# Half tiles for the first block's attention units, all their loads first, and a new order table, in an attention and mixing kernel

## The chip, the cores and the metric

The kernel runs on one core of a Trainium2 chip. The metric is the time of one execution on the device, in microseconds; lower is better. The median of runs is what counts, and one execution under the profiler gives the trace that is read here.

## What is computed

Three stages follow each other on 4 x 576 tokens of 512 features: windowed attention (8 heads of 64, each query sees itself and the 63 positions before it), a token-shift mixer with a squared relu and a sigmoid gate, and a convolution gate of five taps with two more products. All inputs are handed over in 64 bits.

```python
scores = scale * np.matmul(q, k.transpose(0, 1, 3, 2))
scores = np.where((rel >= 0) & (rel < 64), scores, -1e9)
attn = np.exp(scores - max); attn = attn / (sum + 1e-9)
x = attn @ v                                  # (4, 576, 512)
xk = mu_k * x + (1.0 - mu_k) * x_prev         # x_prev: one token back
xr = mu_r * x + (1.0 - mu_r) * x_prev
k = np.maximum(xk @ w_k, 0.0);  v = k * k @ w_v
x = sigmoid(xr @ w_r) * v
gate = sigmoid(causal 5-tap convolution of x with conv_w)
return (gate * (x @ w_val)) @ w_out
```

## The kernel before

**Tiles and stages.** The 2304 tokens are cut into five blocks (`BLOCKS`): block 0 of 256 tokens, blocks 1 to 4 of 512. For each block four attention units, one for each pair of heads, run qk on TensorE (L252, one PSUM buffer for all units), a mask on VectorE (L264), memsets of batch edges on POOL (`edge`, L274), a maximum (`top`, L282), exps with sums on ScalarE (L288), an epsilon add and a reciprocal (L292, L295), a normalization (L297), transposes (L305) and their copies (L311, L312), pv (L318) and a copy into xT (L324, L325). Then `mix` scales xT by mu (L355 on ScalarE or L360 on VectorE) and adds the shifted part with omu = 1 - mu (L371). From block 1 on, x is split into a high and a low part (L385 or L386, L388), and every product (r, h, v; L401) is three matmuls: high by high, high by low, low by high. Block 0 multiplies in one plain pass (L419). After block 4 come val and out, with the convolution taps (L540) on VectorE.

**Weights.** A weight arrives as 64-bit words in 1 MB pieces: two of w_r, four of w_k, four of w_v. `words` makes floats of them: ScalarE L186, a shift on VectorE (L189), a join on VectorE (L191). `weight` then takes the high part (`hi`, L212 on ScalarE or L213 on VectorE) and the rest (`lo`, L215 on VectorE). The first four pieces are loaded by SP (L208), the other six by instructions in ScalarE's queue (L205), each into a buffer that an earlier piece has left. Units load qk (L239) and v (L245) through SP, too; `small` loads mu and the convolution weights.

**What sets the order.** Nothing is reordered at run time: each engine runs its queue in order. Class `Plan` lists operations with a rank, an engine, an estimated duration and dependencies, and lays out a schedule with a model of its own: among the operations that could start on an engine within 130 ns of the earliest, the lowest rank goes first. The ranks come from the table `RANK`. `any` lets an operation go to the engine that ends it first, so a copy or a relu may be on ScalarE, VectorE or POOL. Where TensorE would wait for long early on, `fill` adds idle matmuls (L697). The numbers behind `moves` are the model's transfer times.

**Tiles of the units.** Each unit takes its own tiles qk, vt, s and m from the pool `at2`, which has two buffers of each, also in block 0, where a unit fills only half of one. So unit 2's load of qk waits for unit 0's matmuls (`back("qk", 2)`).

Of the kernel before, what the change touches and what calls it, by code (L numbers as in the profile page):

```python
# [10 lines left out]
I32 = mybir.dt.int32  # L11
# [16 lines left out]
TB = 512  # L28
# [6 lines left out]

RANK = {'first': -349, 'unit': 1, 'mix': -179, 'w_r': -619, 'w_k': -312, 'w_v': -49, 'halves': 300,
        'next': -241, 'nextstep': 74, 'att': -17, 'step': 24, 'inner': 4, 'ahead': 387, 'mixes': -83,
        'mixstep': 56, 'prep': 6, 'gate': 225, 'ldx': 188, 'w2': 65, 'out': 181}


class Plan:
# [5 lines left out]
    START, LAND = 500, 700  # L47
    RAMP, SLOW = 9000, 1.6
    WAIT, PASS = 700, 480
    TABLE = 1280  # L50

    def __init__(self, bias, **rings):

        self.ops, self.bias, self.rings, self.fill = [], bias, rings, None

    def op(self, key, eng, ns, rank, deps, fn, ring=None, table=None, moves=0):

        self.ops.append((rank, len(self.ops), key, ((eng, ns, fn),), deps, ring, table, moves))

    def any(self, key, rank, deps, *ways):  # L60

        self.ops.append((rank, len(self.ops), key, ways, deps, None, None, 0))

    def run(self):
        todo = sorted(self.ops, key=lambda o: o[:2])
        keys = {o[2] for o in todo}
        assert all(d in keys for o in todo for d in o[4])
        end, free, ready = {}, {}, {}
        used = {r: [] for r in self.rings}
        table = None  # L70
        link = 0
        while todo:
            can = {}
            for o in todo[:600]:
                rank, _, key, ways, deps, ring, tab, _ = o
                if key not in ready:
                    if any(d not in end for d in deps):
                        continue
                    ready[key] = max([end[d] + self.HOP for d in deps], default=0)
                t = ready[key]  # L80
# [5 lines left out]
                b = self.bias(rank)  # L86
                w = min(ways, key=lambda w: max(t, free.get(w[0], 0)) + w[1] + b.get(w[0], 0))
                t = max(t, free.get(w[0], 0)) + (self.TABLE if tab and tab != table else 0)
                can.setdefault(w[0], []).append((t, o[:2], o, w))
            assert can, ("no order", [o[2] for o in todo[:8]])  # L90
            t, _, o, w = min((min((c for c in cs if c[0] <= min(cs)[0] + self.SLACK), key=lambda c: c[1])
                              for cs in can.values()), key=lambda c: c[:2])
            _, _, key, _, deps, ring, tab, moves = o
            table = tab or table
            if w[0] == "pe" and self.fill and t - free.get("pe", 0) > self.WAIT:
                self.fill(t, int((t - max(free.get("pe", 0), 1500) - 250) // self.PASS))
            free[w[0]] = t + w[1]
            end[key] = t + w[1]
            if moves:
                link = max(link, end[key] + self.START) + moves * (self.SLOW if link < self.RAMP else 1)  # L100
                end[key] = link + self.LAND
            if ring:
                used[ring[0]].append(ring[1])
            todo.remove(o)
            w[2]()


@with_exitstack
def tile_kernel(ctx, tc, qkh, vh, mu, conv, w_k, w_v, w_r, w_val, w_out, out):
# [84 lines left out]
    def weight(key, rank, w_dram, dst, nm, bufs, prev=None, sprev=None, after=(), free=(), later=None, used=(), queue="dma"):  # L194
# [8 lines left out]
        if queue == "act":  # L203
            op((key, "ld"), "act", 60, rank - 1, [*after, *([(prev, "hi")] if prev else [])],
               lambda: ACT.dma_start(out=bufs()[0], in_=w_dram[key[1]].bitcast(I32)), moves=2.8 * n)  # L205
        else:
            op((key, "ld"), "dma", 420, rank - 1, [*after, *([(prev, "s")] if prev else [])],
               lambda: DMA.dma_start(out=bufs()[0], in_=w_dram[key[1]].bitcast(I32)), moves=2.8 * n)  # L208
        words(key, rank, n, raw, s, [(key, "ld")], [*used, *([(sprev, "lo")] if sprev else [])])
# [15 lines left out]
    def unit(u, r):  # L225
# [20 lines left out]
        op(("ldv", u), "dma", 420, r[3] - RANK["ahead"], back("pv", 2), load_v, moves=3.3 * n)  # L246

# [11 lines left out]
        def mask():  # L259
            s = a["s"] = tile_(at2, "s", [P, 2 * TB // P, P])[:, :2 * n2, :]  # L260
# [487 lines left out]
```

## Time and profile before

| | us |
|---|---|
| median of three runs (455.67 to 456.62) | 456.11 |
| the profiled execution | 454.78 |
| its span, first to last instruction | 453.0 |
| TensorE matmuls busy | 432.6 (95%) |
| VectorE busy | 309.4 (68%) |
| ScalarE busy | 234.3 (52%) |
| POOL busy | 12.2 (3%) |

Times in the views count from the start of the span. A busy share is an average over stages with different limits, so stages are read one by one. A matmul record (PE) ends at a modelled time, and weight loads (PEld) run beside it. Consecutive instructions on VectorE and ScalarE overlap a little: the next one starts before the row of the last has ended.

### The profile page before, as it was taken

The numbers are of one execution on the slowest core, as the hardware profiler recorded it, in microseconds if no ns is written. First come the engines' busy times: TensorE is split into PE (matmuls) and PEld (weight loads), VectorE is DVE, ScalarE is ACT, GpSimd is POOL, SyncE is SP. The second block draws the span as 40 slices with busy tenths as digits, with TensorE's granted clock in tenths as the row PEclk, the third lists the DMA queues.
The fourth block names the chain that finished last, engine by engine and source line by source line (L and its number), as shares of the span: only waits on it lengthen the run. The fifth ranks groups of instructions, "written<-read, shape, count | busy, mean of one in ns | idle before, by whom it ended". The sixth has DMA issues, their size and how long they took to land.

```text
span 453.0 us, 7977 instructions
## 1 busy us (share of the span) xinstructions
PE 432.6 (95%) x3242; PEld 373.0 (82%) x3242; DVE 309.4 (68%) x453; ACT 234.3 (52%) x536; POOL 12.2 (3%) x60
## 2 busy tenths in 40 slices
PE   7687999789999999999999999999999999999996
PEld 5565888678877887878888878888888999999996
DVE  3989999887569215789306946999611899995330
ACT  4667999584758213877046853547400543541122
POOL 2010000000000000001000000000000000000000
PEclk9988999989999999999999999999999999999999
DMA  8994923531113114123121004524041203110122
GB/s 292 415 357 154 341 62 112 167 99 46 48 48 100 48 49 141 51 69 125 69 71 47 1 2 151 186 93 139 1 150 57 95 28 132 53 54 27 52 80 104
DMA packets 16116, 48.90 MB, mean 108 GB/s; under 512 B 1872, under 2 KB 2640, under 8 KB 14800
## 3 DMA queue, kind: packets, MB, share of 16 engines
q1 hardware_dynamic: 15216, 42.10, 27.5%
q10 hardware_dynamic: 864, 6.29, 3.5%
q8 instruction: 25, 0.41, 0.4%
q14 instruction: 11, 0.09, 0.1%
HBM read 38.95 MB, written 9.44 MB: 107 GB/s over the span
## 4 chain that ended last, share of the span: by engine, by line
PE 91%; DVE 5%; issue 1%; ACT 1%; POOL 0%; ACTq 0%; POOLq 0%; DVEq 0%
PE h L401 20%; PE v L401 19%; PE out L401 11%; PE val L401 11%; PE r L401 10%; PE at L318 4%; PE qk L252 4%; PE h L419 3%; PE v L419 3%; PE at L305 3%; PE r L419 1%; PE idle L697 1%; DVE s L264 1%; DVE s L191 1%; DVE m L282 1%
## 5 line engine op out<-in xcount | busy, mean ns | idle before, releaser
L401 PE MATMUL h<-x,wk 128*128 128x512 f32 x384 | 92.4, 395 | 0.0
L401 PEld LDWEIGHTS h<-x,wk 128*128 128x128 f32 x384 | 70.7, 188 | 14.8 <-issue 0.2
L401 PE MATMUL v<-sh,wv 128*128 128x512 f32 x256 | 80.0, 390 | 0.0
L288 ACT ACTIVATE s<-s,m 128x128 f32<-128x128 f32 x144 | 55.7, 388 | 11.1 <-DVE m L282 11.1
L401 PEld LDWEIGHTS v<-sh,wv 128*128 128x128 f32 x256 | 48.1, 188 | 10.0
L401 PE MATMUL val<-x,wk 128*128 128x288 f32 x384 | 52.0, 294 | 0.0
L401 PEld LDWEIGHTS val<-x,wk 128*128 128x128 f32 x384 | 51.2, 188 | 0.1
L540 DVE SCALAR_TENSOR_TENSOR gate<-xb,wc,gate 128x576 f32<-128x576 f32 x64 | 48.8, 810 | 3.3 <-ACT gate L538 3.3
L401 PE MATMUL v<-sl,wv 128*128 128x512 f32 x128 | 49.8, 389 | 0.0
L401 PE MATMUL r<-x,wr 128*128 128x512 f32 x192 | 47.6, 401 | 0.0
L401 PEld LDWEIGHTS r<-x,wr 128*128 128x128 f32 x192 | 35.8, 191 | 7.9 <-issue 0.7
L501 DVE TENSOR_TENSOR sg<-v,sg 128x512 f32<-128x512 f32 (+1 forms) x20 | 12.7, 633 | 40.2 <-PE v L401 36.3
L252 PE MATMUL qk<-qk 64*64 64x128 f32 x576 | 22.5, 296 | 8.6 <-issue 4.5
L312 DVE COPY pt<-at 128x512 f32<-128x512 f32 (+1 forms) x17 | 11.5, 674 | 26.2 <-PE at L305 26.1
L538 ACT ACTIVATE gate<-xb,wc 128x576 f32<-128x576 f32 x16 | 11.2, 765 | 33.3 <-DMA xb<-x2d 33.3
L264 DVE SCALAR_TENSOR_TENSOR s<-qk,cap 128x1024 f32<-128x1024 f32 (+1 forms) x24 | 22.5, 953 | 8.2 <-PE qk L252 8.2
L401 PEld LDWEIGHTS v<-sl,wv 128*128 128x128 f32 x128 | 24.0, 188 | 4.9
L252 PEld LDWEIGHTS qk<-qk 64*64 64x64 f32 x576 | 17.1, 143 | 13.3 <-issue 7.2
L447 ACT ACTIVATE rk<-h 128x512 f32<-128x512 f32 (+1 forms) x29 | 16.2, 565 | 22.6 <-PE h L401 21.4
L288 ACT ACTIVATION_READ_ACCUMULATOR s<-s,m 128x1 f32 x144 | 26.9, 187 | 0.0
L401 PE MATMUL out<-g1h,wk 128*128 128x288 f32 x128 | 26.9, 295 | 0.0
L401 PE MATMUL out<-g0h,wk 128*128 128x288 f32 x128 | 26.9, 295 | 0.0
(113 smaller groups left out, 681.9 us busy)
## 6 DMA issues: line engine op xcount, KB each, us to landing
qk<-qk SPq DMA_DIRECT2D x16, 544.0 KB, 4.6
vt<-vh SPq DMA_DIRECT2D x16, 512.0 KB, 3.8
xb<-x2d SPq DMA_DIRECT2D x4, 1152.0 KB, 5.9
out_t<-o SPq DMA_DIRECT2D x15, 288.0 KB, 2.1
x2d<-sg SPq DMA_DIRECT2D x16, 256.0 KB, 2.0
raw<-w_r SPq DMA_DIRECT2D x2, 1024.0 KB, 8.6
raw<-w_k ACTq DMA_DIRECT2D x2, 1024.0 KB, 8.1
raw<-w_v ACTq DMA_DIRECT2D x2, 1024.0 KB, 7.2
```

The lines of the kernel that those rows point to most:

```text
L252: PE.matmul(a["ps"][heads[c % 2], h, c // 2 * P:c // 2 * P + P], lhsT=a["q"][heads[h], c * W:(c + 1) * W], rhs=a["k"][heads[h], c * W:c * ...
L264: V.scalar_tensor_tensor(out=o, in0=ps[:, i:i + j], scalar=D ** -0.5, in1=cap[:, None, :].to_broadcast([P, j, P]), op0=ALU.mult, op1=ALU.min)
L288: ACT.activation(out=s, in_=s, func=AF.Exp, bias=l(0)[:, c:c + 1], accum_out=l(1)[:, c:c + 1])
L305: PE.transpose(a["tp", h][:, c * P:(c + 1) * P], a["s"][:, h * n2 + c, :], ident)
L312: ("dve", v_ns(n), lambda h=h: V.tensor_copy(a["pt"][:, h, :n], a["tp", h][:, :n])))
L318: PE.matmul(a["o"][heads[h], c * W:(c + 1) * W], lhsT=a["v"][:, c, heads[h]], rhs=a["pt"][:, h, c * W:(c + 1) * W], start=True, stop=True)
L401: PE.matmul(ps, lhsT=a, rhs=b[:, kt, :], start=(kt == 0 and i == 0), stop=(kt == nk - 1 and i == 2))
L419: PE.matmul(Ps[key][:, :n], lhsT=ws(kt), rhs=x()[:, kt, :], start=kt == 0, stop=kt == nk - 1)
L447: ACT.activation(out=o, in_=ps, func=AF.Relu)
L501: V.tensor_tensor(out=s, in0=Ps["v", t, m][:, :n], in1=s, op=ALU.mult)
L538: ACT.activation(out=g, in_=src, func=AF.Copy, scale=c)
L540: V.scalar_tensor_tensor(out=g, in0=src, scalar=c, in1=g, op0=ALU.mult, op1=ALU.add)
```

## The change

The four units of block 0 now share tiles in pairs: `half` gives an even unit a new tile and the odd one its second half, so two buffers hold all four units, and their eight loads wait for nothing. `back2` states the new dependencies: none in block 0; the first two units of block 1 wait for both units of the pair whose tile they take. The tile qk is 64 columns wider, so that two halves fit. mu has a load of its own with rank -1000 that depends on the load of unit 0's v; the convolution weights keep theirs. The planner has lost an unused argument, finds ready operations in another way, and has other constants for transfers. `RANK` has other numbers, and a new table `ADJ` adds a number to the rank of 27 single operations.

```diff
-RANK = {'first': -349, 'unit': 1, 'mix': -179, 'w_r': -619, 'w_k': -312, 'w_v': -49, 'halves': 300,
+RANK = {'first': -329, 'unit': 14, 'mix': -497, 'w_r': -234, 'w_k': -132, 'w_v': 138, 'halves': 542,
...
+ADJ = {('exp', 7): 265, ('mask', 15): -40, ('r', 0, 3): -195, (('w_v', 3), 't'): -390, ('h', 2, 1): 40,
...
-    RAMP, SLOW = 9000, 1.6
+    RAMP, SLOW = 7500, 1.6
...
-        self.ops.append((rank, len(self.ops), key, ((eng, ns, fn),), deps, ring, table, moves))
+        self.ops.append((rank + ADJ.get(key, 0), len(self.ops), key, ((eng, ns, fn),), deps, ring, table, moves))
...
-    def small():
-        DMA.dma_start(out=sm, in_=mu)
-        DMA.dma_start(out=cw, in_=conv.bitcast(I32).rearrange("p (n t) -> p n t", t=2))
-    op("ldc", "dma", 840, -180, [("ldqk", 1)], small, moves=100)
-    op("omu", "dve", 70, -160, ["ldc"],
+    op("ldmu", "dma", 420, -1000, [("ldv", 0)], lambda: DMA.dma_start(out=sm, in_=mu), moves=100)
+    op("ldc", "dma", 420, -180, [("ldqk", 1)],
+       lambda: DMA.dma_start(out=cw, in_=conv.bitcast(I32).rearrange("p (n t) -> p n t", t=2)), moves=100)
+    op("omu", "dve", 70, -960, ["ldmu"],
...
+        def back2(k):
+
+            return [] if t == 0 else [(k, 2 * (u - HP) + i) for i in range(2)] if u < HP + 2 else [(k, u - 2)]
...
+        def half(tag, shape):
+
+            if t:
+                return tile_(at2, tag, shape)
+            if hp % 2 == 0:
+                Q["half", tag] = tile_(at2, tag, shape)
+            return Q["half", tag][:, hp % 2 * shape[1] // 2:]
...
-            both = tile_(at2, "qk", [P, 2 * TB + W])
+            both = half("qk", [P, 2 * TB + 2 * W])
...
-        op(("ldqk", u), "dma", 420, r[0] - RANK["ahead"], back("qk", 2), load_qk, moves=3.2 * n)
+        op(("ldqk", u), "dma", 420, r[0] - RANK["ahead"], back2("qk"), load_qk, moves=2.9 * n)
...
-            a["v"] = tile_(at2, "vt", [P, TB // W, P])
+            a["v"] = half("vt", [P, TB // W, P])
...
-        op(("mask", u), "dve", v_ns(n * 2), r[1], [("qk", u), "cap", *back("mask", 1), *back("tp", 2)], mask)
+        op(("mask", u), "dve", v_ns(n * 2), r[1], [("qk", u), "cap", *back("mask", 1), *back2("tp")], mask)
...
-        l = lambda i: a["m"][:, 8 * i:8 * i + 2 * n2]
+        l = lambda i: a["m"][:, n2 * 2 * i:n2 * 2 * (i + 1)]
```

The order of instructions follows. Names are tiles, the number tells one buffer from another; a count at the end (x2) is of equal rows in a row.

The queue of SP from its start, before: units 0 and 1, then the weights, then unit 2.

```order
L239 DMA qk_129<-qk 128x576
L239 DMA qk_131<-qk 128x576
L245 DMA vt_133<-vh 128x512
L245 DMA vt_135<-vh 128x512
L208 DMA raw_112<-w_r 128x2048
L208 DMA raw_113<-w_r 128x2048
L208 DMA x_110<-w_k 128x2048
L208 DMA s_111<-w_k 128x2048
L239 DMA qk_158<-qk 128x576
L171 DMA sm<-mu 128x8
L172 DMA cw<-conv 128x40
```

The same queue after the change:

```order
L264 DMA qk_110<-qk 128x576 x2
L264 DMA qk_132<-qk 128x576
L270 DMA vt_134<-vh 128x512
L264 DMA qk_132<-qk 128x576
L270 DMA vt_134<-vh 128x512
L270 DMA vt_143<-vh 128x512 x2
L220 DMA raw_114<-w_r 128x2048
L220 DMA raw_115<-w_r 128x2048
L185 DMA cw<-conv 128x40
L220 DMA x_112<-w_k 128x2048
L220 DMA s_113<-w_k 128x2048
L264 DMA qk_180<-qk 128x1088
L183 DMA sm<-mu 128x8
```

The loads of units 2 and 3 have moved ahead of the weights; mu's has moved behind the weights and behind the qk of unit 4 (qk_180).

The queue of ScalarE ahead of the loads of the last two pieces of w_v, before (unit 4's exps are s_424):

```order
L288 ACTIVATE s_424,m_433<-s_424,m_433 128x128 x8
L186 ACTIVATE s_114<-raw_112 128x1024
L488 ACT_TABLE_LOAD
L488 ACTIVATE sg_0_495<-r_0_325 128x256
L186 ACTIVATE s_114<-raw_113 128x1024
L311 ACTIVATE pt_489<-at_498 128x512
L212 ACTIVATE wk_64<-s_114 128x4x256
L488 ACTIVATE sg_1_529<-r_1_337 128x256
L205 DMA raw_112<-w_v 128x2048
```

And after (unit 4's exps stand ten rows above the first of these):

```order
L224 ACTIVATE wk_64<-s_116 128x4x256 x2
L336 ACTIVATE pt_484<-at_519 128x512
L472 ACTIVATE rk_0_490<-h_1_492 128x256
L198 ACTIVATE s_117<-x_112 128x1024
L491 ACTIVATE s_113<-rk_0_490 128x512
L217 DMA raw_114<-w_v 128x2048
L217 DMA raw_115<-w_v 128x2048
```

Both loads now stand together, behind a word step of w_v's first piece (L198, x_112) and a square (L491).

TensorE around v_0 of block 3 (at is a PSUM tile of a transpose or of pv), before:

```order
L305 MATMUL at_2540<-ident,s_2402 128x128 x4
L318 MATMUL at_2550<-pt_2518,vt_2331 64x64 x16
L401 MATMUL v_0_2573<-sh,wv_75 128x512
L401 MATMUL v_0_2573<-sl,wv_75 128x512
L401 MATMUL v_0_2573<-sh,wv_76 128x512
```

And after:

```order
L330 MATMUL at_2484<-ident,s_2114 128x128 x4
L330 MATMUL at_2491<-ident,s_2114 128x128 x4
L343 MATMUL at_2500<-pt_2483,vt_2108 64x64 x16
L330 MATMUL at_2519<-ident,s_2299 128x128 x4
L330 MATMUL at_2527<-ident,s_2299 128x128 x4
L343 MATMUL at_2533<-pt_2518,vt_2314 64x64 x16
L426 MATMUL v_0_2550<-sh,wv_75 128x512
```

Two units' transposes and pv have moved together, between the last h and the first v.

## Rows read from the trace of the kernel before

**Rows 1.** Busy times by stretch; the header names the columns, counts in brackets.

```profile
core 0: us, PE busy (x) PEld busy (x) DVE busy (x) ACT busy (x) POOL busy (x), PEclk, DMA share, GB/s
5.52:93.05 87.53, 74.79 (x790) 62.13 (x794) 80.26 (x127) 68.38 (x192) 4.89 (x28) 0.96 0.66 240
93.84:449.31 355.47, 354.58 (x2425) 308.59 (x2424) 228.15 (x326) 163.16 (x339) 5.41 (x21) 1.00 0.22 74
```

**Rows 2.** VectorE's timeline: start, us, instruction, [idle before and releaser].

```profile
91.83 1.22 DVE L388 TENSOR_TENSOR x<-xm_1r,x 128x1024 fp32r<-128x1024 f32 x1
```

**Rows 3.** VectorE's waits, 0 to 94 us: total, times, longest.

```profile
DVE s L264 <- PE qk L252: 6.5, 3, 4.5
DVE sg L501 <- PE v L419: 1.8, 1, 1.8
DVE pt L312 <- PE at L305: 1.2, 2, 0.7
```

**Rows 4.** TensorE's timeline just ahead of r_0 of block 1.

```profile
91.96 1.88 PE L252 MATMUL qk<-qk 64*64 64x128 f32 x32 [2.73 <-DVE s L264]
```

**Rows 5.** VectorE by line and form, 5 to 94 us: count, busy, mean ns, idle.

```profile
L360 DVE TENSOR_SCALAR x<-xT,sm 128x256 f32<-128x256 f32 x4 | 1.3, 354 | 0.0
L449 DVE TENSOR_SCALAR rk<-h 128x256 f32<-128x256 f32 x4 | 1.6, 431 | 0.4 <-PE h L419 0.4
L292 DVE TENSOR_SCALAR m<-m 128x8 f32<-128x8 f32 x4 | 0.7, 170 | 0.0
L312 DVE COPY pt<-at 128x256 f32<-128x256 f32 x1 | 0.4, 425 | 0.5 <-PE at L305 0.5
...
L215 DVE TENSOR_TENSOR wk<-s,wk 128x1024 fp32r<-128x1024 f32 x4 | 4.9, 1226 | 0.0
L189 DVE TENSOR_SCALAR raw<-raw 128x1024 int32<-128x1024 int32 x6 | 4.1, 688 | 0.0
```

**Rows 6.** VectorE's timeline: units 0 and 1, the last mix, a cast.

```profile
6.51 0.69 DVE L282 TENSOR_REDUCE m<-s 128x4 f32<-128x512 f32 x1 [0.24 <-POOL s L274]
7.57 0.76 DVE L264 SCALAR_TENSOR_TENSOR s<-qk,cap 128x256 f32<-128x256 f32 x2 [0.37 <-PE qk L252]
...
39.22 0.87 DVE L371 SCALAR_TENSOR_TENSOR x<-xT,omu,x 128x256 f32<-128x256 f32 x2
...
77.06 0.69 DVE L213 CAST wv<-s 128x1024 fp32r<-128x1024 f32 x1
77.66 0.17 DVE L292 TENSOR_SCALAR m<-m 128x8 f32<-128x8 f32 x1
```

**Rows 7.** ScalarE by line and form, 5 to 94 us.

```profile
L288 ACT ACTIVATE s<-s,m 128x128 f32<-128x128 f32 x64 | 24.8, 388 | 8.9 <-DVE m L282 8.8
L186 ACT ACTIVATE s<-raw 128x1024 f32<-128x1024 f32 x6 | 7.0, 1174 | 1.0 <-PE r L419 1.0
...
L488 ACT ACT_TABLE_LOAD x1 | 1.3, 1283 | 0.0
```

**Rows 8.** DMA issues: count, KB each, median us from issue to landing.

```profile
raw<-w_v ACTq DMA_DIRECT2D x2, 1024.0 KB, 7.2
```

**Rows 9.** Line L205, the loads issued by ScalarE: from issue to landing.

```profile
DMA to landing us min/median/max: 5.9/8.4/10.1
```

**Rows 10.** TensorE's timeline ahead of v_0 of block 3.

```profile
268.63 0.60 PE L305 MATMUL at<-ident,s 128*128 128x128 f32 x4
...
269.96 1.15 PE L318 MATMUL at<-pt,vt 128*64 128x64 f32 x30 [0.48 <-ACT pt L311]
```

**Rows 11.** The tile sm: its load (ns, first and last start) and landing.

```profile
L171 SPq DMA_DIRECT2D sm<-mu x1: 667/667/667, 5.8 to 5.8; - x1
...
DMA to landing us min/median/max: 12.7/12.7/12.7
```

**Rows 12.** TensorE's timeline: its first long idle time.

```profile
24.21 1.13 PE L252 MATMUL qk<-qk 64*64 64x128 f32 x16 [4.27 <-issue]
```

**Rows 13.** Busy times by stretch, 25 to 30 us, columns as in rows 1.

```profile
25.00:30.00 5.00, 5.00 (x26) 4.01 (x19) 5.00 (x9) 3.30 (x16) 0.84 (x4) 0.77 1.01 425
```

More of the change, by code (lines that the diff above doesn't have):

```diff
@@ L33 @@
 BIG = 3.0e38
-RANK = {'first': -349, 'unit': 1, 'mix': -179, 'w_r': -619, 'w_k': -312, 'w_v': -49, 'halves': 300,
-        'next': -241, 'nextstep': 74, 'att': -17, 'step': 24, 'inner': 4, 'ahead': 387, 'mixes': -83,
-        'mixstep': 56, 'prep': 6, 'gate': 225, 'ldx': 188, 'w2': 65, 'out': 181}
+RANK = {'first': -329, 'unit': 14, 'mix': -497, 'w_r': -234, 'w_k': -132, 'w_v': 138, 'halves': 542,
+        'next': -162, 'nextstep': 48, 'att': -49, 'step': 15, 'inner': 10, 'ahead': 869, 'mixes': -217,
+        'mixstep': 59, 'prep': -542, 'gate': 933, 'ldx': 487, 'w2': -396, 'out': 871}
+ADJ = {('exp', 7): 265, ('mask', 15): -40, ('r', 0, 3): -195, (('w_v', 3), 't'): -390, ('h', 2, 1): 40,
[4 rows of a table added]
+       ('eps', 5): 250, ('tp', 4): 100, ('rec', 1): 540, ('mask', 10): -250}
 class Plan:
@@ L67, in run @@
         assert all(d in keys for o in todo for d in o[4])
-        end, free, ready = {}, {}, {}
+        end, free = {}, {}
+        left, then = {}, {}
+        for o in todo:
+            left[o[2]] = len(set(o[4]))
+            for d in set(o[4]):
+                then.setdefault(d, []).append(o)
+        ready = [(o, 0) for o in todo if not left[o[2]]]
         used = {r: [] for r in self.rings}
@@ L71, in run @@
         link = 0
-        while todo:
+        while ready:
             can = {}
-            for o in todo[:600]:
+            for o, t in ready:
                 rank, _, key, ways, deps, ring, tab, _ = o
[L76 to L80, printed above, removed]
                 if ring and len(used[ring[0]]) >= self.rings[ring[0]]:
@@ L85, in run @@
                     t = max(t, end[last] + self.HOP)
-                b = self.bias(rank)
-                w = min(ways, key=lambda w: max(t, free.get(w[0], 0)) + w[1] + b.get(w[0], 0))
+                w = min(ways, key=lambda w: max(t, free.get(w[0], 0)) + w[1])
                 t = max(t, free.get(w[0], 0)) + (self.TABLE if tab and tab != table else 0)
                 can.setdefault(w[0], []).append((t, o[:2], o, w))
-            assert can, ("no order", [o[2] for o in todo[:8]])
+            assert can, ("no order", [o[2] for o, _ in ready[:8]])
             t, _, o, w = min((min((c for c in cs if c[0] <= min(cs)[0] + self.SLACK), key=lambda c: c[1])
@@ L103, in run @@
                 used[ring[0]].append(ring[1])
-            todo.remove(o)
+            ready = [r for r in ready if r[0] is not o]
+            for c in then.get(key, ()):
+                left[c[2]] -= 1
+                if not left[c[2]]:
+                    ready.append((c, max(end[d] + self.HOP for d in c[4])))
             w[2]()
+        assert len(end) == len(todo), ("no order", [o[2] for o in todo if o[2] not in end][:8])
 @with_exitstack
@@ L204, in weight @@
             op((key, "ld"), "act", 60, rank - 1, [*after, *([(prev, "hi")] if prev else [])],
[L205 removed]
+               lambda: ACT.dma_start(out=bufs()[0], in_=w_dram[key[1]].bitcast(I32)), moves=2.55 * n)
         else:
             op((key, "ld"), "dma", 420, rank - 1, [*after, *([(prev, "s")] if prev else [])],
[L208 removed]
+               lambda: DMA.dma_start(out=bufs()[0], in_=w_dram[key[1]].bitcast(I32)), moves=2.55 * n)
         words(key, rank, n, raw, s, [(key, "ld")], [*used, *([(sprev, "lo")] if sprev else [])])
@@ L276, in unit @@
             op(("edge", u), "pool", 250, r[1], [("mask", u)], edge)
-        l = lambda i: a["m"][:, 8 * i:8 * i + 2 * n2]
+        l = lambda i: a["m"][:, n2 * 2 * i:n2 * 2 * (i + 1)]
         def top():
-            a["m"] = tile_(at2, "m", [P, 16])
+            a["m"] = half("m", [P, 16])
             V.tensor_reduce(out=l(0), in_=a["s"], axis=AX.X, op=ALU.max, negate=True)
-        op(("top", u), "dve", v_ns(n * 2), r[1], [("edge" if firsts else "mask", u), *back("norm", 2)], top)
+        op(("top", u), "dve", v_ns(n * 2), r[1], [("edge" if firsts else "mask", u), *back2("norm")], top)
         def exp():
```

12 lines of the change are left out of this document (6 added, 6 removed), and 4 rows, old and new, of the table ADJ.

## Prediction

> **What bounds the kernel now.** I read the busy times by stretch first. From 93.84 us, where the first three-product matmul of token block 1 (r_0) starts, to 449.31, where the last matmul ends, TensorE is busy 354.58 of 355.47 us: 0.89 us stand idle there [rows 1]. Both kernels issue the same matmuls behind that point, so an edit can win at most 0.9 us behind it and can lose any amount. What is open is when r_0 starts. From VectorE's first mask (5.52) to the end of the instruction that releases r_0 (the low half of xm_1r, L388, 91.83 + 1.22 = 93.05), VectorE is busy 80.26 of 87.53 us [rows 1, 2]; that is 92%, and the remaining 7.3 us are waits: 6.5 for TensorE's qk (4.5 of them before the first mask, outside this stretch), 1.8 for v, 1.2 for transposes [rows 3], and 1.6 in three smaller kinds (an exp sum, POOL's edge memsets, a relu): 6.6 in all, and the rest are gaps of under 0.1 at semaphores. So VectorE's queue sets r_0's start: its work ahead of L388, and its waits. r_0 itself starts 0.79 behind L388, because TensorE first runs a score product (qk) of 1.88 us that had waited for the mask before it [rows 4].
>
> **The change part by part.** It moves work in the first 94 us, adds half tiles, and moves the two small loads.
>
> *VectorE's work ahead of L388.* By the order, the same 10 word conversions, 7 masks, 6 maxima, 5 + 4 norms and 13 weight and x remainders stand ahead of it in both kernels. Gone are four scalings of x (L360, 4 x 0.354, now on ScalarE), two of four relus (L449, 2 x 0.431), one cast (L213, 0.69) and four epsilon adds of 128x8 (L292, 4 x 0.170, now on POOL); new are two copies of 128x256 (2 x 0.425) [rows 5, 6]. A row ends 0.09 after the next one starts (77.06 + 0.69 against 77.66, [rows 6]), so nine instructions fewer count 0.09 less each: 1.42 + 0.86 + 0.69 + 0.68 - 0.85 - 0.8 = **2.0 us less**. On ScalarE this costs 1.7 or so more, which its idle time covers (68.38 busy of 87.53, [rows 1]); on POOL nothing, which is busy 4.89 there.
>
> *VectorE's waits.* The first four units run one behind the other with all their loads in front. Units 0 and 1 keep their waits (0.24 + 0.37 + 0.24 [rows 6]); units 2 and 3 repeat the pattern, which I take as 1.1 for both, and 0.4 for one copy and one mix that follow TensorE and ScalarE directly: 2.35 (an estimate from those gaps). The 1.65 us wait for qk of unit 4, and the later ones for v and the transposes, lose their cause: the loads of units 2 and 3 no longer come behind 4 MB of weights, and VectorE has over ten rows of weight work between unit 3's norm and unit 4's mask.
>
> A new wait takes part of it. The mixes of block 0 end at 40.09 now [rows 6]. Ahead of them the new order has four L189 (4 x 0.60), three L215 (3 x 1.13) and four L360 (1.1) fewer, and 1.3 us less waiting: about 32.0. ScalarE begins the exps of unit 4 at about 30.5, as their maximum ends one mix group earlier, and then goes through 8 exps, a table load, 4 sigmoids, 3 word steps, 2 relus, 2 copies, 2 casts and a square: 3.1 + 1.3 + 1.5 + 3.5 + 0.8 + 1.2 + 2.1 + 0.7 = 14.2 (the first, second and fourth from [rows 7], the others from the same view), less 0.1 of overlap for each of them = 13 us, and only then issues the load of w_v piece 2: at 43.6. VectorE by then has twelve instructions of 1.13, four of 0.60 and two small ones between the mixes and the shift (L189) of that piece, 16.4 us [rows 5]: it stands there at 48.4. The two loads of that kind took 7.2 us at the median, loads issued at that line 5.9 to 10.1 [rows 8, 9]: 50.8, **a wait of 2.4**, which is in front of everything that VectorE does next, and which no row of before shows since its issue at 44.6 was for a shift at 52.8. Its bounds: none (4.8 us to land) to 5.3. Waits in all 2.35 + 2.4 = 4.75 for the 6.6 of before: **1.9 less**.
>
> The trace's 7.2 us stand for loads that shared the engines with qk and vt transfers. The Trainium skill (DMA: Bandwidth & Descriptors, "Anatomy of one DMA") fits a transfer as 2.0 us plus bytes over 436 GB/s; for 1 MB that estimate is 4.4 us, no wait at all, and the sum would be 2.4 lower. No row here shows a 1 MB load that short.
>
> *r_0 behind L388.* In the new order the qk in front of r_0 (now followed by a pv) needs a mask that ends some 4 us before L388 does (a mix of 1.6, a maximum and L388 itself lie between), so r_0 starts with L388: **0.8 less** [rows 2, 4].
>
> *TensorE behind r_0.* The order is changed all the way. At one place I see a new wait: ahead of v_0 of block 3 before runs transpose, h_7, transpose, pv, and waits 0.48 for a copy [rows 10]; the new order has transpose, transpose, pv twice in a row with no h between, so each pv waits for the copy of the transpose right before it and the second unit's second transpose for the copy of the first pv: three waits of some 0.5, **1.0 more** (bounds 0 and 2). I take the tail's val and out steps at no change: VectorE's products there stand in front of their matmuls by 8 us or more in both orders when the same durations are laid along them (an estimate). If that cover were gone, each us late would be one us of TensorE.
>
> *mu, half tiles, POOL.* mu does not load in front of the weights: SP issues it 15th, behind all four weight loads and a 544 KB qk. That is cheap: today it lands at 5.8 + 12.7 = 18.5 [rows 11], and the use of omu on VectorE comes at about 25 in the new order, after five word steps. The pairs share one tile each and add no wait to the masks or exps in the order. SP holds back the ninth and later loads until an earlier one has landed, but eight loads (2.2 MB) are then queued, so the transfers go on. The epsilon adds on POOL cost 0.20 to 0.69 instead of 0.17, ahead of a reciprocal that VectorE reaches later than that in every case I counted.
>
> The Trainium skill (GPSIMD Engine Reference, "Key points") says that POOL shares its SBUF interfaces with VectorE and contends with two-input instructions, which speaks against moving the adds. The trace has no slower VectorE row beside POOL's adds, and with 128x8 elements I put no cost on it.
>
> **Sum**: -2.0 - 1.9 - 0.8 + 1.0 = **-3.7 us**. The profiled execution took 454.78 (span 453.0 and 1.8 around it), so 451.1; the median of the three runs is 456.11, 0.3% above, so the forecast for it is **452.4 us**.
>
> **Rivals.**
> (a) The loads of w_v land in time (4.8 us or less after the issue): -3.7 - 2.4 = -6.1, **450.0**. For it: the queue is emptier by then, as the unit loads went earlier. Against it: no load at that line was faster than 5.9.
> (b) Late loads or a slow clock eat the gain. With the longest landing of that line, 10.1, the wait is 5.3, 2.9 more: **455.3**. The clock can add to it: TensorE was granted 0.77 of full speed at 25 to 30 us, that is 1.2 GHz for a part of it, after it had sat idle for 4.27 us [rows 12, 13]; in the new order it has gaps of 1 to 2 us in 12 to 27 us with fewer idle matmuls in them, and then eight r parts with ScalarE behind them. Half speed there would cost 2 us on ScalarE's issue and so on the wait.
> (c) Slower: mu. omu is queued on VectorE at about 25 us and every mask and word step stands behind it. From a landing at 29 on, 23 us of DMA behind its issue at about 8.5, the whole gain is gone; the DMA engines carry over 400 GB/s until 31 us in before, so at worst it lands there, a wait of 6: -3.7 + 6 = +2.3, **458.4**. Against it: 7 MB stand ahead of it in the new order, 6.3 MB had moved when it landed in before, which is 2 us later.
> (d) The change does not do what it says: for mu that is so, at no cost; for the units it would mean that the first four units still wait for weights, which the issue order excludes.
>
> **How the numbers follow.** Forecast 452.4 (450.8 to 454.2) 0.50; (a) 450.0 (448.3 to 450.8) 0.25; (b) 455.3 (454.2 to 457) 0.13; (c) 458.4, with other waits of TensorE late in the kernel that I have not seen, 0.12. What can be told from no change is 0.2%, 0.9 us: faster is below 455.2. That gives faster 0.50 + 0.25 + half of (b) = 0.82, within 0.2% 0.09, slower 0.09. The range takes the forecast, most of (a) and part of (b): 448.8 to 455.8.
>
> **What would show it.** r_0 of block 1 at about 89 us instead of 93.84, with no qk of 1.9 us right before it; VectorE's shift of w_v piece 2 waiting 1 to 4 us for its load near 50; omu without a wait; VectorE's busy time up to L388 near 78; two or three TensorE waits of half a microsecond ahead of v_0 of block 3. Wrong would be: r_0 at 92 or later (a wait on VectorE that I have not seen), or r_0 early and TensorE idle for over 3 us behind it.

## The result and the profile after

The changed kernel takes 449.86 us (median of four runs, 448.94 to 452.16) where the kernel before takes 455.89 beside it: a ratio of 0.987, 95% interval 0.983 to 0.991. In a second group of runs it was 0.990 (0.988 to 0.992). It is faster by 1.0 to 1.3%, and the time lies inside the range forecast, 2.5 us below the point. The profiled execution took 449.83, with a span of 448.0 for 453.0.

Busy times by stretch of the changed kernel, columns as in [rows 1]. The first stretch runs from the first mask to the end of the low part of xm_1r (L413 now), the second from the first matmul of r_0 to the last matmul of all:

```profile
5.52:87.98 82.46, 75.01 (x783) 60.58 (x783) 77.73 (x118) 68.86 (x191) 7.52 (x32) 0.98 0.70 252
86.15:444.26 358.11, 355.07 (x2428) 308.31 (x2424) 228.40 (x322) 172.42 (x360) 7.55 (x24) 1.00 0.22 75
```

Against [rows 1] the first stretch is 5.07 us shorter: VectorE is busy 77.73 for 80.26 there and idle 4.73 for 7.27. Behind r_0 TensorE now stands idle for 3.04 us, where it was 0.89.

VectorE's waits in the first stretch (total, times, longest); of the 5.6 us for qk, 4.5 lie before the first mask:

```profile
DVE s L289 <- PE qk L277: 5.6, 4, 4.5
DVE raw L201 <- DMA raw<-w_v: 2.1, 2, 1.6
DVE m L307 <- POOL s L299: 0.9, 4, 0.2
DVE pt L337 <- PE at L330: 0.2, 1, 0.2
```

The 1.65 us for unit 4's qk and the 1.8 for v of [rows 3] are gone. In their place stand 2.1 us for the loads of the last two w_v pieces. VectorE's timeline shows them, and below them the gate's low part and the operations that follow it (start, us, instruction, idle before and releaser):

```profile
50.26 0.70 DVE L201 TENSOR_SCALAR raw<-raw 128x1024 int32<-128x1024 int32 x1 [0.56 <-DMA raw<-w_v]
53.71 0.69 DVE L201 TENSOR_SCALAR raw<-raw 128x1024 int32<-128x1024 int32 x1 [1.55 <-DMA raw<-w_v]
...
86.75 1.23 DVE L413 TENSOR_TENSOR x<-xm_1r,x 128x1024 fp32r<-128x1024 f32 x1
...
91.31 1.17 DVE L413 TENSOR_TENSOR x<-xm_1k,x 128x1024 fp32r<-128x1024 f32 x1
92.40 1.22 DVE L322 TENSOR_TENSOR s<-s,m 128x1024 f32<-128x1024 f32 x1
```

The low part of xm_1r starts at 86.75, where it was 91.83 [rows 2]. TensorE around r_0 of block 1, the stretch that answers to [rows 4]:

```profile
84.03 1.10 PE L277 MATMUL qk<-qk 64*64 64x128 f32 x32 [1.72 <-DVE s L289]
...
86.15 6.06 PE L426 MATMUL r<-x,wr 128*128 128x512 f32 x24
93.76 0.63 PE L330 MATMUL at<-ident,s 128*128 128x128 f32 x4 [1.55 <-DVE s L322]
```

Three things are to be seen. The score product takes 1.10 us, not 1.88, and a pv stands between it and r_0. r_0 starts 1.8 us before the low part of xm_1r is there: its first half needs xm_0r alone. And behind r_1 TensorE waits 1.55 us for unit 9's normalization, the L322 row at 92.40 above. In the kernel before, the same stretch reads:

```profile
93.77 6.53 PE L401 MATMUL r<-x,wr 128*128 128x512 f32 x24
100.14 0.60 PE L305 MATMUL at<-ident,s 128*128 128x128 f32 x4
```

So r_1 ends 7.9 us earlier, the transposes behind it only 6.4. From there up to block 3 TensorE does the same matmuls in another order; it waits nowhere in the changed kernel, and once, for 0.32 us, in the kernel before. Ahead of v_0 of block 3 the changed kernel has these rows ([rows 10] before, with one wait of 0.48):

```profile
260.39 0.33 PE L343 MATMUL at<-pt,vt 128*64 128x64 f32 x2 [0.30 <-ACT pt L336]
260.88 1.15 PE L343 MATMUL at<-pt,vt 128*64 128x64 f32 x30 [0.15 <-DVE pt L337]
...
262.87 0.66 PE L330 MATMUL at<-ident,s 128*128 128x128 f32 x4 [0.27 <-DVE xT L349]
...
264.22 1.15 PE L343 MATMUL at<-pt,vt 128*64 128x64 f32 x30 [0.43 <-ACT pt L336]
265.29 0.50 PE L426 MATMUL v<-sh,wv 128*128 128x512 f32 x1
```

Four waits, 1.15 us. v_0 starts 5.75 us earlier than before (271.04), val also 5.7, and the last matmul ends 4.96 earlier.

### The profile page after: what moved, and what is told of

It reads as the page before. It is cut to its first block, busy times and chain, and to the rows that moved or that the text cites. A ratio compares the mean times of both kernels' runs of the same rounds, so it can differ in the third digit from the quotient of the medians.

```text
span 448.0 us, 7939 instructions
## 1 busy us (share of the span) xinstructions
PE 430.7 (96%) x3220; PEld 369.5 (82%) x3220; DVE 304.5 (68%) x438; ACT 241.5 (54%) x546; POOL 17.0 (4%) x67
## 4 chain that ended last, share of the span: by engine, by line
PE 80%; DVE 12%; DMA 4%; ACT 1%; issue 1%; POOL 0%; ACTq 0%; SPq 0%; POOLq 0%; DVEq 0%
PE h L426 20%; PE v L426 19%; PE out L426 11%; PE val L426 9%; PE r L426 9%; PE qk L277 4%; PE at L343 3%; PE at L330 3%; DMA raw<-w_v 2%; PE r L444 2%; DMA xb<-x2d 1%; DVE s L322 1%; DVE x L413 1%; DVE s L289 1%; DVE s L203 1%
## 5 line engine op out<-in xcount | busy, mean ns | idle before, releaser
L426 PE MATMUL h<-x,wk 128*128 128x512 f32 x384 | 91.0, 393 | 0.0
L426 PE MATMUL val<-x,wk 128*128 128x288 f32 x384 | 53.0, 294 | 0.3 <-DVE gv L595 0.3
L472 ACT ACTIVATE rk<-h 128x512 f32<-128x512 f32 (+1 forms) x36 | 19.9, 556 | 22.4 <-PE h L426 21.9
L503 DVE TENSOR_TENSOR sl<-rk,sh 128x1024 fp32r<-128x1024 f32 x16 | 19.6, 1222 | 15.4 <-ACT rk L501 15.2
L612 ACT ACTIVATE o<-out 128x576 f32<-128x576 f32 (+1 forms) x17 | 10.4, 618 | 36.0 <-PE out L426 26.0
L330 PE MATMUL at<-ident,s 128*128 128x128 f32 x144 | 22.8, 282 | 4.3 <-DVE s L322 3.2
```

The lines of the kernel that those rows point to most:

```text
L330: PE.transpose(a["tp", h][:, c * P:(c + 1) * P], a["s"][:, h * n2 + c, :], ident)
L426: PE.matmul(ps, lhsT=a, rhs=b[:, kt, :], start=(kt == 0 and i == 0), stop=(kt == nk - 1 and i == 2))
L472: ACT.activation(out=o, in_=ps, func=AF.Relu)
L503: lambda: V.tensor_tensor(out=Ss[t][1][:, f, :n], in0=rk(), in1=f32(Ss[t][0][:, f, :n]), op=ALU.subtract))
L612: ACT.activation(out=o[:, i], in_=Ps["out", b, h, p][:, i, :HS], func=AF.Copy)
```

## Experiments

Line numbers in the rows of an experiment are those of its own kernel. Where an experiment moves single operations, it lays the changed kernel's order out as a list and moves the operations of `MOVES` ahead of the one named beside them; everything else stays in its order. Times are medians; the kernel before was 455.6 to 456.1 in each group of runs.

**The order tables without the half tiles.** Each unit takes its own tiles again:

```diff
-            if t:
+            if True:
                 return tile_(at2, tag, shape)
...
-            return [] if t == 0 else [(k, 2 * (u - HP) + i) for i in range(2)] if u < HP + 2 else [(k, u - 2)]
+            return back(k, 2)
```

> The changed kernel with its order tables and mu's own load, but every unit takes tiles of its own again, so the loads of units 2 and 3 stand behind four weight loads as before. If the early loads carry the gain: units 2 and 3 are late again, VectorE waits over 6 us ahead of the shift of w_v, and the time is 453 to 457 us, within 0.7% of the kernel before. If the order of single operations carries it whatever the loads do: 449 to 451 us, as the changed kernel (449.9).

**The half tiles and early loads without the tables.** `RANK` and the transfer constants are those of before, `ADJ` is empty:

```diff
-RANK = {'first': -329, 'unit': 14, 'mix': -497, 'w_r': -234, 'w_k': -132, 'w_v': 138, 'halves': 542,
+RANK = {'first': -349, 'unit': 1, 'mix': -179, 'w_r': -619, 'w_k': -312, 'w_v': -49, 'halves': 300,
...
-ADJ = {('exp', 7): 265, ('mask', 15): -40, ('r', 0, 3): -195, (('w_v', 3), 't'): -390, ('h', 2, 1): 40,
+ADJ = {}
```

> The changed kernel's half tiles, loads and mu, but the rank table and the transfer constants of the kernel before and no numbers for single operations. If the early loads carry the gain: 450 to 452 us. If the order of single operations carries it: 453.5 to 456 us. If both are needed, this one and the run with the tables alone both lie within 0.5% of the kernel before (456).

Measured: 461.34 and 459.62, ratios 1.012 (1.010 to 1.015) and 1.008 (1.006 to 1.010). Both are slower than the kernel before, which none of the expectations allowed. r_0 starts at 106.63 with the tables alone, and at 97.00 with the tiles alone, where the rows read:

```profile
88.11 1.17 PE L325 MATMUL at<-ident,s 128*128 128x128 f32 x8 [2.56 <-DVE s L317]
...
95.38 1.69 PE L272 MATMUL qk<-qk 64*64 64x128 f32 x32 [2.57 <-issue]
97.00 6.74 PE L421 MATMUL r<-x,wr 128*128 128x512 f32 x24
```

Neither part carries the gain by itself. With the early loads and the old ranks TensorE has a new wait of 2.6 us for a normalization ahead of r_0, and one of 2.6 ahead of the last score product, where the kernel before has 2.7 [rows 4]. That ranks which fit one set of loads lay out a worse order for another is a reading of the two runs together; it was not followed row by row.

**The loads of w_v earlier.** In ScalarE's queue they go ahead of the casts of w_k pieces 2 and 3:

```diff
+MOVES = [((('w_v', 2), 'ld'), (('w_k', 2), 'hi')), ((('w_v', 3), 'ld'), (('w_k', 3), 'hi'))]
```

> The changed kernel in its own order, with two instructions moved on ScalarE: the loads of w_v pieces 2 and 3 stand ahead of the casts of w_k pieces 2 and 3 (where their buffers come free, near 40.0 and 41.5 us) instead of at 43.6. If the 2.1 us that VectorE waits for them sit on the path: no wait for raw there, the last product of the gate's low part at 84.6 instead of 86.75, time 2.1 lower, 447.7. If something behind it takes the wait's place (ScalarE's exps, or TensorE's work of the first block): 449.0 to 449.9.

Measured: 448.39 (448.03 to 448.90), ratio 0.984 (0.983 to 0.986). Both shifts of w_v now start without a wait:

```profile
50.23 0.69 DVE L212 TENSOR_SCALAR raw<-raw 128x1024 int32<-128x1024 int32 x1
...
52.22 0.69 DVE L212 TENSOR_SCALAR raw<-raw 128x1024 int32<-128x1024 int32 x1
...
85.64 1.22 DVE L424 TENSOR_TENSOR x<-xm_1r,x 128x1024 fp32r<-128x1024 f32 x1
```

The low part of xm_1r starts 1.1 earlier, not 2.1. Two of VectorE's waits (5 to 100 us) show where much of the other microsecond went:

```profile
DVE rk L485 <- PE h L455: 0.3, 1, 0.3
DVE s L501 <- ACT rk L483: 0.3, 1, 0.3
```

These two waits for relus are new. The first stands ahead of the shifts and is part of why the shift at 50.23 is 0.5 later than VectorE was there in the changed kernel (49.7, before its wait of 0.56); the second stands behind them, at 55.4. So the wait for w_v was on the path, and its removal brought 1.1 us at the gate in this execution; the medians give 1.5 to 2.6 against the two of the changed kernel.

**Unit 9's normalization one place earlier.**

```diff
+MOVES = [(('norm', 9), ('xlo', 1, 1, 'k'))]
```

> The changed kernel in its own order, with one instruction moved on VectorE: the normalization of unit 9 ahead of the low part of xm_1k (1.1 us) instead of behind it. TensorE waits 1.55 us for that normalization at 93.76. If this wait gives back part of the gain at r_0: the transposes start 1.1 earlier, at 92.6, and the time is 1.1 lower, 448.7. If the next operation is late in its place (the low part of xm_1k for h_0, or unit 10): 449.5 to 449.9.

Measured: 450.10 (447.58 to 452.19), ratio 0.988 (0.985 to 0.991): no difference from the changed kernel can be told. At its place it did what was expected, the wait is 0.63 for 1.55:

```profile
54.94 0.69 DVE L212 TENSOR_SCALAR raw<-raw 128x1024 int32<-128x1024 int32 x1 [2.27 <-DMA raw<-w_v]
...
87.39 6.02 PE L437 MATMUL r<-x,wr 128*128 128x512 f32 x24
94.03 0.63 PE L341 MATMUL at<-ident,s 128*128 128x128 f32 x4 [0.63 <-DVE s L333]
```

But r_0 itself was 1.24 later in this execution, because the last w_v load came later by as much (its shift starts at 54.94 for 53.71). A change of 1 us can't be read from medians while that wait moves by as much; it has to be tested with the wait taken away (below).

**TensorE kept busy ahead of r_0 in the kernel before.** In the score products of units 10 and 11:

```diff
         def qk():
+            if u in (10, 11):
+                ps = pg.tile([P, TB], F32, tag="g", name=f"busy{u}")
+                for _ in range({10: 3, 11: 11}[u]):
+                    PE.matmul(ps[:, :P], lhsT=ident, rhs=ident, start=True, stop=True)
```

> The kernel before in its own order, with idle matmuls (128x128 on the identity, results unused) on TensorE where it waits ahead of the last two score products before r_0: 3 and 11 of them. They fit into the waits of 0.76 and 2.73 us [rows 4]. If 1.5 us of the gain come from the granted clock (0.52 from 92 to 95.5 us in the kernel before, so that the score product takes 1.88 instead of 1.10 and the 24 matmuls of r_0 and r_1 6.53 instead of some 5.7): the clock stays at 1.0 there, the product takes 1.1, and the time is 1.5 lower, 454.2 for 455.8. If the start of r_0 hangs on the mask in front alone and TensorE makes the time up elsewhere: no change.

Measured: 453.44, ratio 0.9954 (0.9939 to 0.9969), 2.2 us less. The stretch from 92 to 95.5 us of the kernel before, and the same stretch here (columns as in [rows 1]; the number before the DMA share is the granted clock):

```profile
92.00:95.50 3.50, 3.50 (x36) 2.88 (x37) 3.50 (x7) 3.30 (x18) 0.23 (x2) 0.52 0.37 92
```

```profile
92.00:95.50 3.50, 3.50 (x43) 2.91 (x44) 3.50 (x7) 3.30 (x18) 0.22 (x2) 1.00 0.58 176
```

A clock of 0.52 is the lower level, 1.2 GHz, for nearly the whole stretch. TensorE had waited 0.43, 0.76 and 2.73 us before it. Kept busy through the last two of these waits, it stays at 2.4 GHz:

```profile
89.17 2.72 PE L252 MATMUL busy<-ident 128*128 128x128 f32 x22
91.93 1.10 PE L256 MATMUL qk<-qk 64*64 64x128 f32 x32
92.96 5.74 PE L405 MATMUL r<-x,wr 128*128 128x512 f32 x24
98.54 0.60 PE L309 MATMUL at<-ident,s 128*128 128x128 f32 x4
```

The transposes behind r_1 start at 98.54 for 100.14. So 1.6 us of the kernel before at this place were the clock, and the changed kernel has no such stretch there (1.00 from 86.15 to 92.20). The two profiled executions differ by the same 1.6 (453.18 for 454.78). The medians differ by 2.2, since the kernel before's runs of this group go from 454.76 to 456.61 and its profile is one of the shortest; where its longer runs lose the rest no trace shows. (The profile has two rows for each idle matmul.)

**Scalings of block 0 on VectorE.**

```diff
         def scaled():
+            if t == 0:
+                return scaled_v()
```

> The changed kernel in its own order, with the eight scalings of x in block 0 (eight of 128x256) on VectorE instead of ScalarE: some 2.1 us more work on VectorE ahead of the shifts of w_v, and 3.4 less on ScalarE ahead of their loads. If the loads of w_v set VectorE's pace there (2.1 us of waits): the waits go to 0 to 0.5 and the time stays within 0.8 of the changed kernel, 449 to 451. If VectorE's own work counts in full ahead of the gate: 2.1 later, 452.

Measured: 452.58 (450.45 to 455.32), ratio 0.993 (0.991 to 0.996), 1.6 to 2.7 above the two medians of the changed kernel. VectorE's work counted in full: the low part of xm_1r starts 2.7 later than in the changed kernel (89.42), by the 2.1 of work and 0.5 of small new waits for TensorE. The waits for w_v did not shrink:

```profile
DVE raw L201 <- DMA raw<-w_v: 2.1, 2, 1.8
```

The reason is in ScalarE's queue. Its exps of unit 4 now wait 4.37 us for VectorE's maximum and start 1.65 later (32.73 for 31.08). Then it waits 1.0 longer for r of block 0 on TensorE, which is granted 0.50 from 30 to 34 us here, for 0.80 in the changed kernel. So the issue of the two loads (last line, first and last start) moves from 43.6 to 46.2, as far as VectorE moved at the shift of w_v:

```profile
32.73 0.40 ACT L313 ACTIVATE s<-s,m 128x128 f32<-128x128 f32 x1 [4.37 <-DVE m L307]
```

```profile
L217 ACTq DMA_DIRECT2D raw<-w_v x2: 335/610/886, 46.2 to 46.6; - x2
```

**r_0 with the late half first.** On top of the earlier loads:

```diff
-                    gemm(Ps[key][:, :n], wt, [a[:, :, :n] for a in x()], m, range(w * c, w * (c + 1)), nk)
+                    gemm(Ps[key][:, :n], wt, [a[:, :, :n] for a in x()], m,
+                         (2, 3, 0, 1) if key == ("r", 1, 0) else range(w * c, w * (c + 1)), nk)
```

> The run with the earlier loads of w_v (448.4), and r_0 of block 1 takes its four slices of the contraction in the order 2, 3, 0, 1 instead of 0, 1, 2, 3, so that it starts with the half of x that VectorE finishes last, as r_0 in fact did in the kernel before. r_0 then starts at about 86.9 instead of 85.05 and r_1 ends 1.3 later, at 92.4. If the wait for unit 9's normalization (1.59 us behind r_1) swallows an early r_0: that wait shrinks to 0.2 and the time is unchanged, 448.4 within 0.5. If an early r_0 is worth what it shows: 1.3 higher, 449.7.

Measured: 448.10 (447.32 to 448.99) for 448.39: unchanged.

```profile
84.46 0.50 PE L438 MATMUL r<-x,wr 128*128 128x512 f32 x1 [0.54 <-ACT x L421]
85.72 5.55 PE L438 MATMUL r<-x,wr 128*128 128x512 f32 x23 [0.76 <-DVE x L424]
91.46 0.63 PE L341 MATMUL at<-ident,s 128*128 128x128 f32 x4 [0.19 <-DVE s L333]
```

The low part of xm_1r here, and the transposes behind r_1 with the halves in their old order:

```profile
84.44 1.23 DVE L424 TENSOR_TENSOR x<-xm_1r,x 128x1024 fp32r<-128x1024 f32 x1
```

```profile
92.66 0.63 PE L341 MATMUL at<-ident,s 128*128 128x128 f32 x4 [1.59 <-DVE s L333]
```

r_0 waits for its operands now, and the wait behind r_1 shrinks from 1.59 to 0.19. This execution is 1.2 us ahead all along. Counted from the end of the low part, r_1 ends after 5.6 us, where it ended after 4.2 with the late half last: 1.4 is what the early start brings. It is given back in full at unit 9's normalization.

**Three moves together, first form.**

```diff
+MOVES = [((('w_v', 2), 'ld'), (('w_k', 2), 'hi')), ((('w_v', 3), 'ld'), (('w_k', 3), 'hi')),
+         (('norm', 9), ('xlo', 1, 1, 'k')), (('tp0', 9), ('tp', 9)), (('pt', 9, 0), ('pt', 9, 1)),
+         (('tp0', 18), ('h', 3, 6)), (('pt', 18, 0), ('relu', 3, 6)), (('tp', 18), ('h', 3, 7)), (('pt', 18, 1), ('xhi', 4, 0, 'k')), (('pv', 19), ('v', 3, 1, 0)), (('x', 19), ('v', 3, 1, 0))]
```

> The changed kernel in its own order with three things moved: the two loads of w_v earlier (448.4 by itself); unit 9's normalization ahead of the low part of xm_1k and its transposes behind r_2 instead of r_1 and r_2; and ahead of v_0 of block 3 the transposes of unit 18 between h_5, h_6 and h_7 and pv of unit 19 behind the first part of v_0. If the waits on TensorE that the changed kernel has behind r_0 (1.55 at unit 9, 1.15 ahead of v_0 of block 3) are lost time: 2.4 lower than 448.4, 446.0. If other waits take their place: 447.5 to 448.4.

Measured: 444.67. In this form two mixes of block 4 were issued ahead of the copy of unit 19's values and did not use them, so it does not compute the same thing and its time stands only for comparison. The second form keeps pv of unit 19 in its place and moves units 18 and 19 ahead instead:

```diff
-         (('tp0', 18), ('h', 3, 6)), (('pt', 18, 0), ('relu', 3, 6)), (('tp', 18), ('h', 3, 7)), (('pt', 18, 1), ('xhi', 4, 0, 'k')), (('pv', 19), ('v', 3, 1, 0)), (('x', 19), ('v', 3, 1, 0))]
+         (('tp0', 18), ('h', 3, 4)), (('pt', 18, 0), ('relu', 3, 4)), (('tp', 18), ('h', 3, 5)), (('pt', 18, 1), ('slo', 3, 1)),
+         (('pv', 18), ('h', 3, 6)), (('x', 18), ('slo', 3, 2)), (('tp0', 19), ('h', 3, 6)), (('pt', 19, 0), ('relu', 3, 6)),
+         (('tp', 19), ('h', 3, 7)), (('pt', 19, 1), ('relu', 3, 7))]
```

> The changed kernel in its own order with three things moved: the loads of w_v as in the run that moved them alone (448.4); unit 9's normalization ahead of the low part of xm_1k and its transposes behind r_2; in block 3 the transposes and pv of unit 18 and the transposes of unit 19 between h_3 and h_7, each with an h behind it, and pv of unit 19 in its old place ahead of v_0. As the run before it with the same first two moves, 444.7, if its 3.7 us behind 448.4 came from the waits on TensorE: 444.3 to 445.5. If a part of it came from the mix of block 4 that did not wait for unit 19 there: 445.5 to 446.5.

Measured: 444.95 (443.82 to 446.06), ratio 0.9765 (0.9747 to 0.9783), 3.4 below the run with the earlier loads alone. TensorE around r_0:

```profile
84.54 8.74 PE L441 MATMUL r<-x,wr 128*128 128x512 f32 x36
93.12 1.04 PE L345 MATMUL at<-ident,s 128*128 128x128 f32 x8
```

The wait at unit 9 is gone. Between the start of r_0 and h_0 lie 13.4 us (84.54 to 97.93) where the run with the earlier loads has 15.2 (85.05 to 100.23): 1.8 for the 1.59 of the wait. From h_0 to v_0 of block 3 it is 1.95 us less, more than the 1.15 us of waits there; the other 0.8 was not followed. So both waits behind r_0 were lost time, and nothing took their place.

**The changed kernel once more, and TensorE kept busy at 26 us.** Two runs, the second with

```diff
                 if c == 0:
+                    if key == ("r", 0, 0):
+                        for _ in range(8):
+                            PE.matmul(idle["ps"][:, :P], lhsT=ident, rhs=ident, start=True, stop=True)
```

> The changed kernel itself, unedited, beside the other runs of this group: 449.9 as in its first runs (448.9 to 452.2), with the same waits of VectorE for w_v, between 2 and 3 us in all. If the landing of these two loads makes its runs differ, they spread over 3 us or more, against 0.9 in the run with the earlier loads.

> The changed kernel in its own order, with eight more idle matmuls (128x128 on the identity, results unused) on TensorE ahead of the first part of r in block 0, where it stands idle for 1.69 us at 26.0 and is granted 0.66 of its clock from 27 to 32 us afterwards. If that half clock holds up ScalarE (0.84 us of its waits are for r there) and so the issue of the w_v loads: the clock stays at 1.0, the issue comes 0.8 earlier than 43.6, and the time is 0.8 lower, 449.1. If VectorE alone sets that part, by way of the mixes and the maximum that ScalarE waits for: no change, 449.9.

Measured: 450.95 (449.80 to 453.23) unedited, 450.58 (449.06 to 452.58) with the idle matmuls: not to be told apart. The granted clock from 27 to 32 us, of the changed kernel in its first profile and of the edited one:

```profile
27.00:32.00 5.00, 4.35 (x39) 3.22 (x40) 5.00 (x10) 3.98 (x12) 0.26 (x3) 0.66 0.99 390
```

```profile
27.00:32.00 5.00, 4.60 (x52) 3.62 (x51) 5.00 (x10) 3.98 (x11) 0.23 (x2) 1.00 0.97 380
```

The clock rises, the issue of the w_v loads comes 0.3 earlier (43.3), and the time does not move. The unedited run's profile shows how far one kernel's executions differ: the loads issued at 44.5, 3.0 us of waits for them, r_0 at 89.41 for 86.15, and much the same wait behind r_1 (1.57):

```profile
89.41 6.04 PE L426 MATMUL r<-x,wr 128*128 128x512 f32 x24
97.02 0.63 PE L330 MATMUL at<-ident,s 128*128 128x128 f32 x4 [1.57 <-DVE s L322]
```

The last w_v load made VectorE only 1.8 us later than in the first profile (its shift starts at 55.54 for 53.71). By the rows, most of the other 1.4 is TensorE's clock. TensorE waits for the normalization that stands behind that load in VectorE's queue. Four rows show it: the transposes behind that wait in the first profile and in this one, this one's clock there, and a wait of VectorE that follows:

```profile
55.68 1.23 PE L330 MATMUL at<-ident,s 128*128 128x128 f32 x8 [1.39 <-DVE s L322]
```

```profile
57.52 1.94 PE L330 MATMUL at<-ident,s 128*128 128x128 f32 x8 [2.29 <-DVE s L322]
```

```profile
57.00:61.00 4.00, 3.48 (x14) 2.82 (x14) 3.47 (x7) 2.10 (x5) 0.16 (x2) 0.57 0.04 15
```

```profile
63.72 0.69 DVE L337 COPY pt<-at 128x512 f32<-128x512 f32 x1 [0.73 <-PE at L330]
```

Idle for 2.29 us instead of 1.39, TensorE was granted 0.57 from 57 to 61, where the first profile has 1.00 (55 to 59). VectorE waits 0.53 and 0.73 for its transposes, which it does not in the first profile. So a late load can cost more than its lateness.

The unedited kernel's runs spread over 3.4 us, as expected if the landing moves them, and the earlier loads' over 0.9. The second form of the three moves spreads over 2.2 with early loads too, so the landing is not the whole of it.

**The moves and the idle matmuls.**

> The run with the three moves, and the eight idle matmuls ahead of the first part of r. With the loads of w_v off the path, a faster r reaches VectorE by the relus and copies only: 0 to 0.5 lower. If TensorE's clock at 27 to 32 us sets the pace there in its own right: 1.0 to 1.7 lower.

Measured: 444.14 (443.77 to 444.45), ratio 0.9745 (0.9732 to 0.9759). This is the fastest version of the study, 11.9 us below the kernel before and 5.7 to 6.8 below the changed kernel. The step from 444.95 is within the spread of that run; what of it the idle matmuls bring is not settled.

## Why the prediction was right, and where its steps failed

The sum said -3.7 us and the profile shows -5.0; five of its six steps missed by half a microsecond or more, partly against each other.

| step | forecast | measured |
|---|---|---|
| VectorE's work ahead of the low part of xm_1r | -2.0 | -2.5 |
| VectorE's waits | -1.9 | -2.5 |
| r_0 and r_1 behind that low part | -0.8 | -2.9 |
| directly behind r_1 | 0 | +1.55 |
| ahead of v_0 of block 3 | +1.0 | +0.6 |
| val and out | 0 | +0.75 |
| sum | -3.7 | -5.0 |

The mechanism up to the gate was right: VectorE's queue set r_0's start, and its work and waits ahead of the low part fell. That the total came near is in part luck, since 2.1 us too little at r_0 stand against 2.3 of losses behind r_1 and in the tail that the sum put at nothing. The point forecast was 2.5 us too high for two reasons of about equal size, some 1.3 each: the sum, and the step from the profiled execution to the median. I took the median 0.3% above the profile, as it was in the kernel before; here the profile (449.83) is at the median (449.86). The time lies in the range because the range took in rival (a).

*VectorE's work.* Right, short by 0.5. The rows that went and came are those of the forecast, with six maxima of 128x1024 ahead of the low part in both kernels. The rows' durations add up to 3.3 us less, 2.8 of it from these rows, and overlap between rows takes 0.8 of it again, as forecast. The other 0.5 is that rows of the same kind were slightly shorter in this profile (the four remainders of w_k 1.204 us on average for 1.226 [rows 5]); why, no run shows. The eight scalings put back bear out that such work counts in full: 2.1 us of work, and the low part 2.7 later, 0.5 of it new waits.

*Waits.* Near in sum, partly by luck. The load issue (43.6) came out to the tenth because unit 4's exps started 0.6 later than forecast (31.08 for 30.5) and what follows them took 0.5 less. The wait for w_v was forecast at 2.4, all of it for the first load, and measured at 2.1, in two parts. For the first load it is 0.56: VectorE came at 49.7, not 48.4, and the load took 6.6 us to land where I took 7.2 [rows 8]. I gave the second no thought; it took 9.7, and VectorE waited 1.55 for it. The four first units cost 2.0 for the 2.35 of the estimate: 1.1 for qk, 0.7 for POOL's edges, 0.2 for a transpose. Gaps of under 0.1 shrank by another 0.3. The Trainium skill (DMA: Bandwidth & Descriptors, "Anatomy of one DMA") has a fit, measured on the gpsimd path and not on the queues of SP and ScalarE that these loads take, by which 1 MB would be some 4.4 us, an estimate. The measurements lie above it: the 1 MB loads of the changed kernel took 6.3 to 13.6, and the shortest of all runs, 4.75, is in the run with the w_v loads moved earlier.

*r_0 behind the low part.* This step failed in size. I read the 1.88 us of the score product [rows 4] as its length and took 0.8 for its move. It is 1.10 long; TensorE was at 1.2 GHz after its wait of 2.73, and the first half of r_0 and r_1 was slow as well. The run with idle matmuls shows 1.6 us for it. The row that would have told me is in [rows 1] and beside it: the first stretch reads 0.96, and I read the clock at 25 to 30 us alone [rows 13], not at 92. The other 1.3 us come from the first half of r_0, which needs xm_0r only and now starts ahead of the gate; with the halves reversed, 1.4 us of it are gone.

*Behind r_1.* I forecast nothing here, on the ground that TensorE is busy all the way; yet the last of the signs that I had named for being wrong, an early r_0 and over 3 us idle behind it, came true by a hair (3.04). A TensorE that comes 8 us earlier meets a VectorE that comes 5 earlier: unit 9's normalization stands behind the gate, a mix, a copy, a maximum and another low part in VectorE's queue. The reversed halves of r_0 show that this wait swallows what r_0's early start had won, and the three moves together that it is lost time.

*Block 3 and the tail.* The three waits of half a microsecond were there, as four smaller ones of 1.15 in all, for 0.8 in the kernel before (0.32 and 0.48); the other 0.3 of the step I have not traced. In val and out I took the cover of 8 us as safe; val waits once for 0.34, and the rest of 0.4 I have not traced to rows.

*mu.* As forecast: it landed 13.2 us after its issue at 8.7, and omu ran at 25.91 without a wait:

```profile
25.91 0.17 DVE L187 TENSOR_SCALAR omu<-sm 128x8 f32<-128x8 f32 x1
```

*POOL.* The epsilon adds held VectorE up nowhere by as much as 0.1 us, as forecast, and no VectorE row beside them is slower. But one of them took 1.36 us where most take 0.20, while VectorE ran a remainder of 1.22 us with two inputs, and it ended just as VectorE came to the reciprocal behind it (36.19):

```profile
34.80 1.36 POOL L317 TENSOR_SCALAR m<-m 128x8 f32<-128x8 f32 x1
```

*Rivals.* (a) had the right time, 450.0, for a wrong reason: the loads did not land in time. (b) was half there: the half clock at 27 us appeared, yet removing it changed nothing that the runs can tell; in the second profile of the changed kernel both of its parts show, a load that lands later and a lower clock behind it, and cost that execution some 3 us. (c) did not happen. Rival (d) is answered in part: the early loads do what they say, but without the new order they make the kernel slower.

## What to carry to other kernels

A row that is longer than its twins is first a question about the granted clock in that very stretch: a wait on TensorE can cost more than its length, since what follows it may run at half speed. When an edit lets one engine run ahead of another by more than that other gains, look down the slower one's queue for the next thing the fast one needs; the gain stops there until that is moved too. And loads and order belong together: here each alone lost 0.8 to 1.2%, both together won 1.0 to 1.3%, and moving some fifteen operations by hand along the waits that the trace still showed won as much again.

## What was not expected of the hardware

The half clock does not follow from the idle time alone. TensorE stood idle for 1.69 us at 26 us in the changed kernel and was then granted 0.66 from 27 to 32; in the run with the three moves it stood idle for 1.68 in the same place and kept 1.00. The changed kernel's second profile reads 0.80 behind the same 1.69. The rows of the run with the three moves:

```profile
28.23 1.13 PE L459 MATMUL r<-x,s 128*128 128x256 f32 x4 [1.68 <-DVE x L411]
29.76 1.10 PE L292 MATMUL qk<-qk 64*64 64x128 f32 x32 [0.40 <-DVE s L304]
```

The score product behind that gap took 1.99 us in the changed kernel's first profile, 1.60 in its second and 1.10 here. What decides between them these runs do not show.
